# Routing operands moved into the columns that the attention products leave free in their PSUM banks, and routing constants issued one by one

## The chip, the cores and the metric

The kernel runs on one core of one Trainium2 chip. The metric is the device time of one execution in microseconds (us); the kernel before takes 656.65 us, the median of three runs (655.53, 656.65, 656.81). TensorE (PE) does the matmuls, VectorE (DVE) and ScalarE (ACT) the elementwise work, GpSimd (POOL) part of the pooling and the indirect DMAs, SyncE (SP) issues the other DMAs.

## What is computed

Two layers, one behind the other. Attention with keys and values that are averaged in groups of 8, for 8 batches, 8 heads, 576 positions of 64 elements; then a mixture of experts (MoE) in which every one of the 4608 tokens goes to its best expert of 8.

```python
k_p = k.reshape(B, H, Sp, pool, D).mean(axis=3)          # 576 -> 72 keys
v_p = v.reshape(B, H, Sp, pool, D).mean(axis=3)
scores = scale * np.matmul(q, k_p.transpose(0, 1, 3, 2))
attn = softmax(scores)
x = (attn @ v_p) with the heads side by side             # 4608 x 512
logits = x @ w_gate + modality_bias[modality_id]         # 4608 x 8
e_idx = np.argmax(logits, axis=1)
gate_w = softmax(logits)[np.arange(N), e_idx]
for e in range(8):
    mask = e_idx == e
    h = np.maximum(x[mask] @ w1[e], 0.0)                 # 512 -> 1024
    out[mask] = gate_w[mask, None] * (h @ w2[e])         # 1024 -> 512
```

## The kernel before

**Attention.** The tokens are 36 tiles of 128, worked off in 20 steps (`steps`): four steps out of five take two tiles, and the mixed step takes one tile that holds the last 64 tokens of two batches. The main loop (L882 to L955) issues the steps as a software pipeline. In step n it finishes the tiles of step n - 1 (`old`), makes the second half of the scores of step n and the first half of step n + 1. The parts are

- `q_pe`, `q_act` (L480, L494): the queries are transposed by TensorE and copied by ScalarE.
- `s_pe` (L498), `s_dve` (L518), `s_act` (L529): the scores in PSUM; VectorE takes their maximum `mx` (L522) and the difference `sb` (L525); ScalarE takes the exponentials (L537, L538).
- `t_pe`, `t_act`, `t4_pe`, `t4_act` (L540 to L563): the probabilities are transposed and copied to `pt` and `pt4`. In program order `s_act(n, 0)` stands ahead of `t4_act(n - 1)` on ScalarE.
- `a_pe` (L565): the products with the pooled values (L579 and L583), for four heads into each of two PSUM banks `av0` and `av1`. Each value has a column of ones and the gate's weights beside it, so that the sums and the gate's logits come out too. 292 of a bank's 512 columns are used.
- `x_dve` (L585): for each bank u the sum (L599), its reciprocal (L601), the normalised output `xb` (L603) and the logits of each head `lg` (L605).
- `v_gate` (L370): the gate columns of the values, two TensorE lines (L378, L379) and three VectorE lines.

Functions that a step owes now and then (the pooling of the next batch, the splits of the weights, the start of a routing group) hang in `hook_0` to `hook_3` by step.

**Routing.** After every nine tiles a group is routed: `route(g)` (L635) is a list of about 24 small VectorE operations, and then nine `arow` (L706), which compare a row 0 to 127 (`iota_b`) with each token's place. In it are `lgr` (the logits, L653 to L662), `ex` on ScalarE (L659), the count `dc` (L680), a chain of matmuls that adds up the places (`pe`, L671 to L675), and `rs` (L695 or L698). These operations wait in a list `drip`, and `gap(n)` (L458) issues the next n of them at fixed places inside `s_dve` and `x_dve`; `release()` issues one that holds TensorE work. Behind group 0 comes `first_expert` (L709), behind group 1 `early_table` (L746). Group 3 is routed after the attention, in the first slot of the MoE; its `arow` stand in `late[0, 5]` (L1062).

**Constants.** `routing_constants_2` (L422) makes 11 VectorE constants in one block at the end of step 3 (L950): `idt`, `idw`, `mf` (L430, which reads the modality words `mod`), `mq`, `bias_all` and `b1` (which read `mb`), `w8`. Both are loaded by SP in step 1 (`load_routing`, L398 to L403); GpSimd pools keys and values at the same time (L296 to L298).

**MoE.** Up to 27 slots of 256 tokens, 19 of them filled here. `first` (L159) makes a block of hidden units in a PSUM tile `hp` (TensorE L163, ScalarE L165, VectorE L167 for the residual `hlo`), `second` (L1101) the output products (L1108). fp32 operands are split into a high and a low part, with three products. The tiles `hp` take the banks of `av0` and `av1` (L970). At the end of slot 0, at f = 7, `first_next` (L1124) makes the first block of slot 1 in `hp[0]`.

All tiles are under a framework that puts semaphore waits between engines wherever their accesses of a tile depend on each other; for PSUM it does so by bank.

Of the kernel before, what the change touches and what calls it, by code (L numbers as in the profile page):

```python
# [30 lines left out]
def kernel(  # L31
# [152 lines left out]
    with ExitStack() as actx:  # L184
# [237 lines left out]
        def routing_constants_2():  # L422
            mod, mb, ids, idt = RC["mod"], RC["mb"], RC["ids"], RC["idt"]
            nc.vector.tensor_single_scalar(idt, ids, 6, op=ALU.logical_shift_right)
            nc.vector.tensor_copy(idw[:, 0, :], idt)
            nc.vector.tensor_single_scalar(idt, ids, 63, op=ALU.bitwise_and)
            nc.vector.tensor_scalar_add(idw[:, 1, :], idt, 1.0)
# [2 lines left out]
            nc.vector.tensor_copy(mf, mod[:, :, 0])  # L430
# [3 lines left out]
            nc.vector.tensor_tensor(bias_all, mq[:, 0, :].rearrange("p (t o) -> p t o", o=1).to_broadcast([P, NT, E]),
                                    mb[:, 0:1, :].to_broadcast([P, NT, E]), op=ALU.mult)
            nc.vector.tensor_tensor(b1, mq[:, 1, :].rearrange("p (t o) -> p t o", o=1).to_broadcast([P, NT, E]),
                                    mb[:, 1:2, :].to_broadcast([P, NT, E]), op=ALU.mult)
            nc.vector.tensor_add(bias_all, bias_all, b1)

            nc.vector.tensor_scalar(w8, iota_f[:, 0:E], -1.0, float(E), op0=ALU.mult, op1=ALU.add)  # L440
# [124 lines left out]
        def a_pe(t):  # L565
# [69 lines left out]
        def route(g):  # L635
# [6 lines left out]
            m2 = small("m2", g, [P, n])
            sm = small("sm", g, [P, n])
            dc = small("dc", g, [P, E])
            rs = small("rs", g, [P, n, E])
            rk = small("rk", g, [P, n])
            rki = small("rki", g, [P, n], I32)
            rkm = small("rkm", g, [P, n], I32)
            rkf = small("rkf", g, [P, n])
# [55 lines left out]
            for i in range(n):  # L705
                add(lambda i=i: V.tensor_scalar(arow[:, t0 + i, :], iota_b, rkf[:, i:i + 1], None, op0=ALU.is_equal))  # L706
            return ops

        def first_expert():  # L709
# [172 lines left out]
        for n in range(N + 1):  # L882
# [354 lines left out]
```

## Time and profile before

| | before |
|---|---|
| median of three runs | 656.65 us (655.53 to 656.81) |
| the profiled execution | 655.7 us, span 654.0 us |
| mean granted TensorE clock | 0.983 |
| busy PE, DVE, ACT, POOL | 94%, 67%, 52%, 30% |
| first output product of the MoE (L1108) | at 202 us |
| ranges of TensorE waits of 1.8 us or more between 45 and 206 us | 3.02, 1.86, 1.83, 1.86, 2.04 us |

The span runs from the first to the last instruction; the execution's time is 1.7 us longer. Times below are microseconds from the span's start. In a row of single instructions stand start, duration, engine, line, operation, output <- input, elements, the count of instructions in the row and, in brackets, the wait just before it and what ended it. In a row of a stretch stand the busy times of PE, PEld (the weight load), DVE, ACT and POOL, then the clock that TensorE was granted (1.00 is full).

### The profile page before, as it was taken

The page shows a single profiled execution, that of the slowest core. Times are in us where ns is not written, and L with a number is a line of the kernel's source. Part 1 is how long each engine was busy: PE and PEld are TensorE (multiplying, and loading weights), DVE is VectorE, ACT ScalarE, POOL GpSimd, SP SyncE. Part 2 cuts the span into 40 slices and gives each one's busy share as a digit, 9 for nine tenths or more (in the row PEclk, how much of TensorE's full clock was granted, in tenths as well). Part 3 has the DMA queues.
Part 4 walks back from the last instruction along what each step waited for, and adds up shares of the span by engine and source line. Part 5 has one row for each costly group of instructions (what it writes and reads, how often), then busy time and mean ns, then how long its engine had stood idle before and what let it go on. Part 6 is the DMA issues. An engine that isn't in the chain of part 4 may idle for free.

```text
span 654.0 us, 12681 instructions
## 1 busy us (share of the span) xinstructions
PE 616.0 (94%) x4313; PEld 558.6 (85%) x4313; DVE 438.6 (67%) x963; ACT 340.9 (52%) x625; POOL 193.6 (30%) x239
## 2 busy tenths in 40 slices
PE   4898898899799999999999999999999999999993
PEld 3697798789698999999999999999999999999982
DVE  4878888999987666665665666566566656656530
ACT  2674574478451354454555555555555555555530
POOL 5698744661100121311211212320221221122121
PEclk9998898899999999999999999999999999999997
DMA  9999978473411821202102253201215410120120
GB/s 253 289 279 353 354 220 285 143 241 108 126 28 58 258 82 51 67 1 67 55 15 64 88 185 117 65 33 35 67 50 176 163 55 17 51 66 17 51 72 15
DMA packets 63484, 77.15 MB, mean 118 GB/s; under 512 B 15535, under 2 KB 42159, under 8 KB 63408
## 3 DMA queue, kind: packets, MB, share of 16 engines
q1 hardware_dynamic: 57168, 55.98, 27.9%
q0 software_dynamic: 6240, 20.26, 9.6%
q8 instruction: 36, 0.59, 0.4%
q14 instruction: 40, 0.33, 0.2%
HBM read 119.94 MB, written 19.71 MB: 214 GB/s over the span
## 4 chain that ended last, share of the span: by engine, by line
PE 73%; DVE 12%; DMA 8%; issue 4%; ACT 1%; SPq 0%; POOL 0%; POOLq 0%; DVEq 0%; ACTq 0%
PE op L1108 27%; PE hp L163 27%; DMA out_dram<-ob,sidx 7%; PE av L579 4%; PE sc L515 3%; PE xt L154 2%; PE av L583 2%; DVE mx L522 2%; DVE sb L525 2%; PE ph L163 2%; PE pp L544 1%; PE pq L490 1%; DVE hl L139 1%; PE ptab L1014 1%; DMA k<-in_k_dram 1%
## 5 line engine op out<-in xcount | busy, mean ns | idle before, releaser
L136 ACT CAST hl<-raw 128x1024 fp32r<-128x1024 f32 x138 | 144.8, 1049 | 143.0 <-PE op L1108 140.0
L163 PE MATMUL hp<-xh,hl 128*128 128x256 f32 x1152 | 186.0, 284 | 0.6 <-issue 0.6
L163 PEld LDWEIGHTS hp<-xh,hl 128*128 128x128 f32 x1152 | 166.1, 189 | 11.6 <-issue 1.0
L139 DVE TENSOR_TENSOR hl<-raw,hl 128x1024 fp32r<-128x1024 f32 x144 | 174.9, 1216 | 0.0
L1108 PE MATMUL op<-hl,hh 128*128 128x512 f32 x556 | 174.2, 394 | 0.0
L1094 POOL DMA_INDIRECT out_dram<-ob,sidx x38 | 52.7, 1387 | 376.6 <-DVE ob L1090 267.1
L167 DVE SCALAR_TENSOR_TENSOR hlo<-hp,hh 128x256 fp32r<-128x256 f32 x139 | 58.9, 424 | 139.8 <-ACT hh L165 134.9
L1108 PE MATMUL op<-hl,hlo 128*128 128x512 f32 x278 | 108.8, 392 | 0.0
L1108 PEld LDWEIGHTS op<-hl,hh 128*128 128x128 f32 x556 | 95.2, 189 | 12.2
L163 PE MATMUL hp<-xl,hl 128*128 128x256 f32 x576 | 92.0, 282 | 0.0
L165 ACT ACTIVATE hh<-hp 128x256 fp32r<-128x256 f32 x139 | 53.4, 384 | 49.6 <-PE hp L163 47.6
L163 PEld LDWEIGHTS hp<-xl,hl 128*128 128x128 f32 x576 | 79.0, 190 | 0.0
L1108 PEld LDWEIGHTS op<-hl,hlo 128*128 128x128 f32 x278 | 52.2, 188 | 11.8
L579 PE MATMUL av<-vw,pt 128*128 128x146 f32 (+1 forms) x320 | 52.7, 306 | 1.8 <-DVE lg L605 1.5
L143 POOL DMA_INDIRECT xg<-xs,gidx x40 | 43.5, 1088 | 17.7 <-issue 9.2
L579 PEld LDWEIGHTS av<-vw,pt 128*128 128x128 f32 (+1 forms) x320 | 42.2, 190 | 4.1 <-DVE lg L605 2.8
L515 PE MATMUL sc<-kt,qt 128*128 128x144 f32 x256 | 40.0, 303 | 1.9 <-DVE sb L525 1.8
L522 DVE TENSOR_REDUCE mx<-sc 128x8 f32<-128x576 f32 (+1 forms) x40 | 27.7, 693 | 17.6 <-ACT pt L563 10.9
L515 PEld LDWEIGHTS sc<-kt,qt 128*128 128x128 f32 x256 | 35.8, 203 | 2.5 <-issue 2.0
L157 DVE TENSOR_TENSOR xl<-xt,xh 128x512 fp32r<-128x512 f32 x38 | 24.6, 686 | 17.6 <-ACT xh L156 17.6
L549 ACT COPY pt<-pp 128x512 f32<-128x512 f32 x36 | 21.1, 585 | 29.1 <-PE pp L544 28.5
L583 PE MATMUL av<-vw,pt 128*128 128x146 f32 (+1 forms) x160 | 31.2, 298 | 0.5 <-ACT pt L563 0.5
(226 smaller groups left out, 725.7 us busy)
## 6 DMA issues: line engine op xcount, KB each, us to landing
raw<-in_moe_w_dram SPq DMA_DIRECT2D x304, 256.0 KB
xs<-xb SPq DMA_DIRECT2D x16, 528.0 KB
k<-in_k_dram SPq DMA_DIRECT2D x7, 1024.0 KB
v<-in_v_dram SPq DMA_DIRECT2D x7, 1024.0 KB
q<-in_q_dram SPq DMA_DIRECT2D x6, 1024.0 KB
q<-in_q_dram SPq DMA_DIRECT2D x4, 512.0 KB
v<-in_v_dram SPq DMA_DIRECT2D x16, 128.0 KB
xs<-xb SPq DMA_DIRECT2D x8, 132.0 KB
```

The lines of the kernel that those rows point to most:

```text
L136: nc.scalar.copy(hl[f][:, 0, :], raw[f])
L139: eng.tensor_sub(hl[f][:, 1, :], raw[f], hl[f][:, 0, :].bitcast(F32))
L143: nc.gpsimd.indirect_dma_start(out=xgs[(2 * s + tt) % len(xgs)], out_offset=None, in_=xs[0:rows, :], in_offset=IndirectOffsetOnAxis(idx[:, ...
L163: nc.tensor.matmul(ph, hl[f][:, w, d * P:(d + 1) * P], x[:, d, :], start=(n == 0 and d == 0), stop=(n == 2 and d == ND - 1))
L165: nc.scalar.activation(hh, ph, AF.Relu)
L167: nc.vector.scalar_tensor_tensor(hlo, ph, 0.0, hh.bitcast(F32), op0=ALU.max, op1=ALU.subtract)
L515: nc.tensor.matmul(dst, qt[:, i, :], kt[b % NB][:, :, h * SPL:(h + 1) * SPL], start=True, stop=True)
L522: nc.vector.reduce_max(mx, scv, axis=AX.X)
L579: nc.tensor.matmul(av[u][hs, 2 * VC * gg:2 * VC * (gg + 1)], pt[:, c, hs], vw[y][:, c].rearrange("p a x -> p (a x)"), start=(gg == 0), sto ...
L583: nc.tensor.matmul(dst4[hs], pt4[:, hs], v4[y][:, 2 * u:2 * u + 2, :], start=False, stop=True)
L1094: nc.gpsimd.indirect_dma_start(out=out[:, :], out_offset=IndirectOffsetOnAxis(idx.bitcast(U32), 0), in_=ob, in_offset=None, bounds_check=N ...
L1108: nc.tensor.matmul(o[tt], l[:, ts_], hl[f][:, w, D:2 * D], start=(f == 0 and n == 0), stop=(f == NF - 1 and n == 2))
```

## The change

`av0` and `av1` are allocated once and stay (`av_bank`); the products and the MoE's `hp` use them directly. A helper `place(u, shape)` cuts tiles from columns 292 to 511 of bank u. In `av0` then lie `iota_q` (fp32, in place of the bf16 `iota_b`; copied by VectorE from `iota_f` at the start, where GpSimd cast it before), `m2`, `sm`, `rk`, `rki`, `rkm` and `dc`; in `av1` lie `e0oh`, `lg` (the group's logits, `lgr` before), `rs`, `rot` and the early table's `s0`; its `b1` uses the columns of `rs`. `first_expert` gets a second tile `rots` in SBUF and one copy more. The eleven constants become a list that `hook_0` hangs behind `drip` in step 3.

```diff
+    AVW = 4 * VC
+    av_bank = [ps_av.tile([P, 512], F32, name=f"av{u}") for u in range(2)]
+    taken = [AVW, AVW]
+    def place(u, shape, dt=F32):
+        n = 1
+        for x in shape[1:]:
+            n *= x
+        c = taken[u]
+        taken[u] += n
+        assert taken[u] <= 512
+        a = av_bank[u][:, c:c + n]
+        if dt != F32:
+            a = a.bitcast(dt)
+        return a if len(shape) == 2 else a.rearrange("p (t e) -> p t e", e=shape[2])
...
-    iota_b = cp.tile([P, P], BF16, name="iota_b")
-    nc.gpsimd.tensor_copy(iota_b, iota_f)
+    iota_q = place(0, [P, P])
+    nc.vector.tensor_copy(iota_q, iota_f)
...
-    e0oh = cp.tile([P, E], F32, name="e0oh")
+    e0oh = place(1, [P, E])
...
         def routing_constants_2():
...
+            return [
+                lambda: V.tensor_single_scalar(idt, ids, 6, op=ALU.logical_shift_right),
...
+                lambda: V.tensor_copy(mf, mod[:, :, 0]),
...
-            av = [ps_av.tile([P, 512], F32, tag=f"av{u}", name=f"av_{t}_{u}") for u in range(2)]
+            av = av_bank
...
+        RQ = {k: place(1, [P, GT, E]) for k in ("lg", "rs")}
+        RQ.update((k, place(0, [P, GT])) for k in ("m2", "sm", "rk"))
+        RQ.update((k, place(0, [P, GT], I32)) for k in ("rki", "rkm"))
+        RQ.update(dc=place(0, [P, E]))
...
+            lg, rs, m2, sm, dc, rk, rki, rkm = (RQ[k] for k in ("lg", "rs", "m2", "sm", "dc", "rk", "rki", "rkm"))
...
-                add(lambda i=i: V.tensor_scalar(arow[:, t0 + i, :], iota_b, rkf[:, i:i + 1], None, op0=ALU.is_equal))
+                add(lambda i=i: V.tensor_scalar(arow[:, t0 + i, :], iota_q, rkf[:, i:i + 1], None, op0=ALU.is_equal))
...
-            rot = ap.tile([P, E], F32, name="rot")
+            rot = place(1, [P, E])
+            rots = ap.tile([P, E], F32, name="rots")
...
-                lambda: V.tensor_add(rot, rot, t8),
-                lambda: V.tensor_tensor(lmat, rot.rearrange("p (o e) -> p o e", o=1).to_broadcast([P, E, E]),
+                lambda: V.tensor_add(rots, rot, t8),
+                lambda: V.tensor_copy(rot, rots),
+                lambda: V.tensor_tensor(lmat, rots.rearrange("p (o e) -> p o e", o=1).to_broadcast([P, E, E]),
                                         rot.rearrange("p (e o) -> p e o", o=1).to_broadcast([P, E, E]), op=ALU.is_lt),
...
-            s0 = ap.tile([P, T], F32, name="s0")
+            s0 = place(1, [P, T])
...
-            b1 = ap.tile([P, C, T], BF16, name="b1")
+            b1 = RQ["rs"].rearrange("p t e -> p (t e)").rearrange("p (c t) -> p c t", c=C)
...
+        at(hook_0, 3, lambda: drip.extend(routing_constants_2()))
...
-            if n == 3:
-                routing_constants_2()
...
-    hp = [ps_av.tile([P, 512], F32, tag=f"av{i}", name=f"hp{i}") for i in range(2)]
+    hp = av_bank
```

The order of instructions moves in one place. On VectorE, around the end of step 3, the constants stood in a block between `sb` of step 4's first half and `mx` of its second half (the last two constants are left out; what a row waits for stands in brackets, DMAHW are DMA queues):

```order
L605 TENSOR_TENSOR lg_429<-av_1_641,r_1_674 128x32
L522 TENSOR_REDUCE mx_0_694<-sc_0_682 128x8 [waits PE_49]
L525 TENSOR_TENSOR sb_0_696<-sc_0_682,mx_0_694 128x576 [waits DVE_49]
L424 TENSOR_SCALAR idt<-ids 128x36
L425 CAST idw<-idt 128x36 [waits DVE_49]
L426 TENSOR_SCALAR idt<-ids 128x36 [waits DVE_49]
L427 TENSOR_SCALAR idw<-idt 128x36 [waits DVE_49]
L430 CAST mf<-mod 128x36 [waits DMAHW2_49,DMAHW7_49,DMAHW1_49,DMAHW0_49]
L432 TENSOR_SCALAR mq<-mf 128x36 [waits DVE_49]
L432 TENSOR_SCALAR mq<-mf 128x36
L434 TENSOR_TENSOR bias_all<-mq,mb 128x288 [waits DMAHW3_49,DVE_49]
L436 TENSOR_TENSOR sc_107<-mq,mb 128x288 [waits DVE_49]
```

On the same engine and at the same place, the changed kernel issues (`av_72` is bank `av1`; lines are the changed file's own, 26 higher here in the tile functions):

```order
L625 TENSOR_SCALAR r_1_670<-av_72 128x4 [waits PE_49]
L457 CAST mf<-mod 128x36 [waits DMAHW2_49,DMAHW7_49,DMAHW1_49,DMAHW0_49]
L627 RECIPROCAL r_1_670<-r_1_670 128x4 [waits DVE_49]
L458 TENSOR_SCALAR mq<-mf 128x36 [waits DVE_49]
L629 TENSOR_TENSOR xb_169<-av_72,r_1_670 128x256 [waits DVE_49]
L631 TENSOR_TENSOR lg_427<-av_72,r_1_670 128x32
L459 TENSOR_SCALAR mq<-mf 128x36
L450 TENSOR_TENSOR bias_all<-mq,mb 128x288 [waits DMAHW3_49,DVE_49]
L548 TENSOR_REDUCE mx_0_694<-sc_0_682 128x8 [waits PE_49]
L450 TENSOR_TENSOR sc_107<-mq,mb 128x288 [waits DVE_49]
L462 TENSOR_TENSOR bias_all<-bias_all,sc_107 128x288 [waits DVE_49]
L551 TENSOR_TENSOR sb_0_698<-sc_0_682,mx_0_694 128x576
```

`mf`, with its wait for the four loads of the modality words, has moved from behind `sb` of step 4 into the normalisation of the tile before it; four earlier constants stand above these rows, in the second half of step 3.

Elsewhere the order stays, and the waits change. On TensorE, at the end of slot 0 of the MoE, the first block of slot 1 (`hp`) before:

```order
L1108 MATMUL op_1_2881<-hl_2412,h_6_2773 128x512 x3
L163 MATMUL hp_2884<-xh_2875,hl_1766 128x256 [waits DMAHW3_49,DMAHW2_49,DMAHW7_49,DMAHW1_49,Activation_49]
L163 MATMUL hp_2884<-xh_2875,hl_1766 128x256 x3
L163 MATMUL hp_2884<-xl_2876,hl_1766 128x256 [waits DVE_49]
L163 MATMUL hp_2884<-xl_2876,hl_1766 128x256 x3
```

And in the changed kernel on the same engine (`av_71` is bank `av0`):

```order
L1133 MATMUL op_1_2776<-hl_2329,h_6_2680 128x512 x3
L182 MATMUL av_71<-xh_2770,hl_1709 128x256 [waits DMAHW2_49,DMAHW3_49,DMAHW1_49,DMAHW7_49,DVE_49,Activation_49]
L182 MATMUL av_71<-xh_2770,hl_1709 128x256 x3
L182 MATMUL av_71<-xl_2771,hl_1709 128x256 x4
L182 MATMUL av_71<-xh_2770,hl_1709 128x256 x4
```

The block's first matmul waits for VectorE now: the last VectorE instruction that touches bank `av0` ahead of it is the last `arow`, which reads `iota_q`.

More of the change, by code (lines that the diff above doesn't have):

```diff
@@ L422, in routing_constants_2, with biased @@
         def routing_constants_2():
+            V = nc.vector
             mod, mb, ids, idt = RC["mod"], RC["mb"], RC["ids"], RC["idt"]
[L424 to L427, printed above, removed]
             mf = ap.tile([P, NT], F32, name="mf")
             mq = ap.tile([P, 2, NT], F32, name="mq")
-            nc.vector.tensor_copy(mf, mod[:, :, 0])
-            for m in range(2):
-                nc.vector.tensor_single_scalar(mq[:, m, :], mf, float(m), op=ALU.is_equal)
             b1 = sc1
[L434 to L440, printed above, removed]
+            def biased(m, dst):
+                V.tensor_tensor(dst, mq[:, m, :].rearrange("p (t o) -> p t o", o=1).to_broadcast([P, NT, E]),
+                                mb[:, m:m + 1, :].to_broadcast([P, NT, E]), op=ALU.mult)
+            return [
+                lambda: V.tensor_single_scalar(idt, ids, 6, op=ALU.logical_shift_right),
+                lambda: V.tensor_copy(idw[:, 0, :], idt),
+                lambda: V.tensor_single_scalar(idt, ids, 63, op=ALU.bitwise_and),
+                lambda: V.tensor_scalar_add(idw[:, 1, :], idt, 1.0),
+                lambda: V.tensor_copy(mf, mod[:, :, 0]),
+                lambda: V.tensor_single_scalar(mq[:, 0, :], mf, 0.0, op=ALU.is_equal),
+                lambda: V.tensor_single_scalar(mq[:, 1, :], mf, 1.0, op=ALU.is_equal),
+                lambda: biased(0, bias_all),
+                lambda: biased(1, b1),
+                lambda: V.tensor_add(bias_all, bias_all, b1),
+                lambda: V.tensor_scalar(w8, iota_f[:, 0:E], -1.0, float(E), op0=ALU.mult, op1=ALU.add),
+            ]
         steps = []
@@ L638, in route @@
             sl = slice(t0, t0 + n)
-            lg = small("lgr", g, [P, n, E])
             ex = small("ex", g, [P, n, E])
+            rkf = small("rkf", g, [P, n])
             m1 = small("m1", g, [P, n])
[L642 to L649, printed above, removed]
+            lg, rs, m2, sm, dc, rk, rki, rkm = (RQ[k] for k in ("lg", "rs", "m2", "sm", "dc", "rk", "rki", "rkm"))
             V = nc.vector
```

## The prediction

> **What bounds the kernel now.** I read the page first, then TensorE's busy time and clock by stretches, then the waits and single instructions at the places where TensorE stops. The page's TensorE row and five stretches (start:end, length, busy time of PE, PEld, DVE, ACT, POOL, granted clock, DMA share, GB/s):
>
> ```profile
> PE 616.0 (94%) x4313; PEld 558.6 (85%) x4313; DVE 438.6 (67%) x963; ACT 340.9 (52%) x625; POOL 193.6 (30%) x239
> ...
> 62.00:70.00 8.00, 8.00 (x68) 7.67 (x66) 6.64 (x22) 5.89 (x17) 5.03 (x10) 1.00 1.06 352
> 70.00:80.00 10.00, 7.93 (x50) 6.15 (x49) 9.71 (x34) 3.56 (x11) 9.21 (x10) 0.83 1.06 351
> 101.00:110.00 9.00, 7.17 (x47) 6.85 (x46) 7.78 (x32) 4.44 (x11) 2.07 (x2) 0.81 0.75 255
> 172.00:182.00 10.00, 7.35 (x76) 6.51 (x76) 9.70 (x29) 2.93 (x7) 0.00 (x0) 1.00 0.17 56
> 182.00:203.00 21.00, 21.00 (x172) 20.82 (x172) 15.81 (x60) 9.58 (x24) 0.00 (x0) 1.00 0.13 40
> ```
>
> TensorE carries the time: where it is full (62 to 70, 182 to 203) a microsecond lost is a microsecond at the end. It loses time in short stretches, where VectorE is nearly full and the clock falls to about 0.8: (1 - 0.83) x 10 and (1 - 0.81) x 9 are 1.7 us of clock each. TensorE's first matmuls after its long waits (start, duration, line; in brackets the wait and its releaser):
>
> ```profile
> 54.77 0.63 PE L378 MATMUL sc<-wgb,vt 128*128 128x32 f32 x4 [3.02 <-DVE sb L525]
> 73.73 0.63 PE L378 MATMUL sc<-wgb,vt 128*128 128x32 f32 x4 [1.86 <-DVE sb L525]
> 103.10 1.64 PE L515 MATMUL sc<-kt,qt 128*128 128x144 f32 x6 [1.83 <-DVE sb L525]
> 119.24 0.63 PE L378 MATMUL sc<-wgb,vt 128*128 128x32 f32 x4 [1.86 <-DVE sb L525]
> 178.65 0.73 PE L163 MATMUL ph<-xl,hl 128*128 128x256 f32 x4 [2.04 <-DVE xl L157]
> ```
>
> I call the first four S1, S2, S3 and S4. Why VectorE is late there (per line: ns minimum/median/maximum; then one GpSimd instruction):
>
> ```profile
> L654 DVE TENSOR_TENSOR lgr<-lgr,bias_all x4: 232/1314/2400, 70.6 to 204.6; 128x72 f32<-128x72 f32 x4
> ...
> 70.57 2.34 POOL L296 TENSOR_TENSOR v<-v 128x1024 f32<-128x1024 f32 x1
> ...
> L706 DVE TENSOR_SCALAR arow<-iota_b,rkf x36: 218/243/3051, 100.7 to 215.2; 128x128 bf16<-128x128 bf16 x36
> L603 DVE TENSOR_TENSOR xb<-av,r x72: 409/424/425, 27.3 to 202.6; 128x256 f32<-128x256 f32 x72
> L698 DVE TENSOR_TENSOR rs<-sc,oh x2: 222/222/222, 88.0 to 133.2; 128x72 f32<-128x72 f32 x2
> ```
>
> L654 has both inputs in SBUF and takes 232 ns or 2400: at 70.6 it stands as long as GpSimd's L296. L603, with one input in PSUM, never passes 425 ns in 72 runs, under the same GpSimd work. So operations on the moved operands should not be held at S2 to S4. The sum hangs on what their place in the products' banks and the new issue order make wait instead.
>
> **The constants (S1): +3.3.** They keep their SBUF operands, so only their places change. In order: the DMA packets of 47.5 to 48.0, then VectorE, ScalarE and TensorE.
>
> ```profile
> DMA packets 23, 0.00 MB, mean 1 GB/s; under 512 B 23, under 2 KB 23, under 8 KB 23
> ...
> 45.29 0.76 DVE L522 TENSOR_REDUCE mx<-sc 128x8 f32<-128x576 f32 x1 [0.38 <-PE sc L515]
> 46.08 0.76 DVE L525 TENSOR_TENSOR sb<-sc,mx 128x576 f32<-128x576 f32 x1
> 49.86 0.50 DVE L430 CAST mf<-mod 128x36 f32<-128x36 int32 x1
> 52.20 0.46 DVE L438 TENSOR_TENSOR bias_all<-bias_all,sc 128x288 f32<-128x288 f32 x1
> ...
> 46.90 0.64 ACT L537 ACTIVATE pe<-sb 128x512 f32<-128x512 f32 x1
> 47.58 0.56 ACT L563 COPY pt<-sc 64x128 f32<-64x128 f32 x2
> ...
> 48.14 0.41 PE L583 MATMUL av<-vw,pt 128*128 128x146 f32 x2
> 51.15 0.60 PE L490 MATMUL pq<-ident,q 128*128 128x128 f32 x4
> ```
>
> Before, mf (L430) runs at 49.86, when the modality words are there. Now it stands inside the normalisation of step 3, which VectorE reaches at about 44.6 (before, it ended there 0.38 ahead of mx at 45.29). The words travel in packets under 512 B, and the last of these still move in the slice 47.5 to 48.0, so mf waits until about 48.2. Behind it in VectorE's queue stand the rest of that normalisation, five more constants and mx and sb of step 4. From mf to L438 before are 52.66 - 49.86 = 2.8 us; with 0.6 for the rest of the normalisation (L603's 0.42 and small ones) and 1.5 for mx and sb (0.76 as L525, twice), sb ends at about 53.1 instead of 46.84: 6.3 late. ScalarE takes the exponentials of sb (L537) before its copy L563, so that copy is 6.3 late too, and TensorE's L583, which reads it, goes at about 54.4 instead of 48.14. From there to the end of L490 before are 51.75 - 48.14 = 3.6 us; TensorE passes L490 at 58.1, where before it had waited until 54.77. That is +3.3. With no GpSimd in the way three wide constants take 0.46 each, as L438, and three narrow ones no more than L698's 0.22: 2.0 instead of 2.8, and the price is +2.5; held by as much again, +4.1. If the words came by 44.6, the constants would fill waits such as the 0.38 before mx, and TensorE's wait would shrink by something between 0.4 and its 3.02; I take -1.2, nearer the first. The slow clock that followed the old wait follows the new one instead.
>
> **Group starts (S2, S4): -0.2 each.** The count dc (VectorE), and TensorE's next products:
>
> ```profile
> 76.48 0.28 DVE L680 TENSOR_REDUCE dc<-oh 128x8 f32<-128x72 bf16 x1
> ...
> 74.83 0.77 PE L579 MATMUL av<-vw,pt 128*128 128x146 f32 x4
> ```
>
> L654 falls from 2.40 to 0.23: 2.2 us earlier on VectorE, and the matmuls of L378 go 1.9 earlier. But dc now lies in the bank that the products at 74.83 write, and they wait for it. It moves from 76.76 to 74.6, less than 0.2 us before those products went anyway. TensorE's wait moves from before L378 to behind it. If the clock then holds, up to 1.9 each.
>
> **The first expert (S3): -3.0.**
>
> ```profile
> 95.23 1.27 DVE L724 TENSOR_TENSOR t<-e0oh,iota_f 128x8 f32<-128x8 f32 x1
> 97.99 0.67 DVE L727 TENSOR_SCALAR rot<-iota_f,e 128x8 f32<-128x8 f32 x1
> 98.69 0.65 DVE L728 TENSOR_SCALAR t<-rot 128x8 f32<-128x8 f32 x1
> 100.72 1.57 DVE L706 TENSOR_SCALAR arow<-iota_b,rkf 128x128 bf16<-128x128 bf16 x2
> ```
>
> At 0.2 us each, the first three give back 2.0 and the two arows 1.1; the added copy takes 0.1. So sb is 3.0 earlier. TensorE's wait of 1.83 goes but for 0.5 in which the products ahead wait for an arow, and the slow clock behind it, 1.7, goes too. Bounds: 1.3 if the clock falls all the same, 3.5 if nothing waits.
>
> **Group 1's arows: -1.2.**
>
> ```profile
> 138.69 3.21 DVE L706 TENSOR_SCALAR arow<-iota_b,rkf 128x128 bf16<-128x128 bf16 x2
> ```
>
> VectorE gains 2.8. None of TensorE's long waits lies there, so I take less than half; bounds 0 and 2.8.
>
> **Groups 2 and 3: +0.4, +1.5, +2.8.** GpSimd is nearly idle by then, so nothing is gained, and new waits remain (TensorE and ScalarE at group 2's start; then rs, TensorE's products, the residual and TensorE's transposes; then the MoE's first hidden block and the last arows):
>
> ```profile
> 162.32 0.69 PE L579 MATMUL av<-vw,pt 128*128 128x146 f32 x4
> 164.38 0.26 ACT L659 ACTIVATE ex<-lgr 128x72 f32<-128x72 f32 x1 [2.56 <-DVE m L655]
> ...
> 179.18 0.22 DVE L695 TENSOR_TENSOR rs<-sc,adjv 128x72 f32<-128x72 f32 x1
> 181.09 0.42 PE L583 MATMUL av<-vw,pt 128*64 128x146 f32 x4
> 184.97 0.42 DVE L167 SCALAR_TENSOR_TENSOR h<-ph,h 128x256 fp32r<-128x256 f32 x1
> 185.79 0.60 PE L544 MATMUL pp<-ident,pe 128*128 128x128 f32 x4
> ...
> 212.92 0.63 PE L163 MATMUL hp<-xh,hl 128*128 128x256 f32 x4
> 213.87 1.54 DVE L706 TENSOR_SCALAR arow<-iota_b,rkf 128x128 bf16<-128x128 bf16 x9
> ```
>
> The products at 162.32 wait for ex, which reads the logits in their bank and ends at 164.64. That holds TensorE 2.3, but VectorE is the bound here; its next read of that bank must wait for these products (0.69 long): +0.4 (0 to 1.1). At 179.18 rs must now wait for the products that end at 181.51: 2.3 on VectorE. The transposes that wait for the residual went 0.4 after its end at 185.39, so at most 1.9 late; VectorE is idle a quarter of 182 to 203, so up to 1.5 of the six microseconds between may swallow it: +1.5 (0.4 to 1.9), near the top, since that idle time need not fall there. At 212.92 the MoE's hidden block takes the bank in which iota_q lies, so TensorE waits for the last arow, which ends at 215.41. From L698 to L603 an element from PSUM costs (409 - 222) / (256 - 72) = 1.02 ns, so an arow from there takes 222 + 56 x 1.02 = 279 ns, 0.06 over L706's minimum; nine of them end 0 to 0.5 later: +2.8 (2.5 to 3.0). The slow clock followed four of the five waits above (not the last, in whose stretch it is 1.00); I charge half of 1.7, +0.8 (0 to 1.7). [...]
>
> Everything else is hidden: iota_q's copy lies under the first loads, GpSimd's missing cast under its own queue, the early table's wait under the wait at 162.32.
>
> **Sum**: 3.3 - 0.2 - 0.2 - 3.0 - 1.2 + 0.4 + 1.5 + 2.8 + 0.8 = +4.2. The profiled run took 655.7 (span 654.0), so 659.9; from the median of 656.65 it is 660.85. I take 660.4, and add 0.5 to the profiled run's sums below alike.
>
> **The rivals.**
> Faster: the release of dc at S2 and S4. If it comes so early that TensorE's wait there falls well under the 1.83 us after which the clock fell, the clock holds and each place gives 3.5 instead of 0.2: 4.2 - 6.6 = -2.4, 653.8. For it: VectorE is 2.2 earlier. Against it: dc stands last in the group's first block.
> No change: the modality words come before mf. Then S1 is -1.2 instead of +3.3: -0.3, 655.9. Against it: the packets of 47.5 to 48.0.
> The change doesn't do what it says: an operand in PSUM waits for GpSimd all the same. S2 to S4 and group 1 give nothing: 4.2 + 4.6 = +8.8, 665.0. L603's maximum speaks against it.
> PSUM is dearer for VectorE: some 23 small operations of groups 2 and 3, on a path there, each cost the 0.06 more that the arow's estimate gives: +1.4, 661.8. Against it: 72 elements take 222 ns with PSUM (L698) and 232 without (L654's minimum). [...]
>
> **The numbers.** Chances: forecast 0.60 (657.5 to 663), no loss at dc 0.14, early words 0.12, PSUM still held 0.07, PSUM dearer 0.07. The range 655.2 to 665.0 leaves out the faster rival and the forecast's tails, 0.19. About 0.2%, 1.3 us, is what a measurement of this kernel can tell from no change. Faster is the first rival and 0.03 of tail, 0.17; same the early words and 0.03, 0.15; slower the rest, 0.68.
>
> **What would show it.** Right: mf starting at about 48 after an idle VectorE; TensorE idle from 48 to about 54; L654 and the arows never above 0.5 us; TensorE's first hidden block behind the last arow. Wrong: mf at 45 without a wait, clock 1.00 in the stretches of S2 and S4, or the hidden block of slot 0 starting at once.

## The result and the profile after

The changed kernel takes 664.18 us, the median of four runs (662.88 to 666.5); the kernel before takes 656.51 beside it (655.53 to 656.81). The ratio is 1.0114, interval 1.0077 to 1.0151: slower by 7.7 us, where 3.75 were forecast. The profiled execution took 664.43 us, span 662.7, mean granted clock 0.980.

Single runs scatter with the clock: in 35 runs beside the first experiments the kernel before took 651.49 to 661.15 us, the fastest at 0.986, the slowest at 0.975. So the ratios carry the verdicts, and the traces, one for each kernel, the causes. In experiment 7 two of ten runs (667.57 and 667.67) were slow ones and are left out.

The page's engine row of the changed kernel: TensorE has the same 4313 instructions and 2.6 us less busy time than before, VectorE 10.8 less. The kernel does not work more, it waits more.

```profile
PE 613.4 (93%) x4313; PEld 555.9 (84%) x4313; DVE 427.8 (65%) x965; ACT 340.5 (51%) x625; POOL 193.2 (29%) x238
```

TensorE's first matmuls after its new waits, from the timeline of the changed kernel (start, duration; the wait and what ended it in brackets):

```profile
55.11 0.85 PE L609 MATMUL av<-vw,pt 128*128 128x146 f32 x2 [5.38 <-ACT pt L589]
79.22 0.52 PE L605 MATMUL av<-vw,pt 128*128 128x146 f32 x2 [2.15 <-DVE av L703]
104.19 0.77 PE L605 MATMUL av<-vw,pt 128*128 128x146 f32 x4 [0.97 <-DVE arow L729]
122.61 0.64 PE L605 MATMUL av<-vw,pt 128*128 128x146 f32 x3 [2.15 <-DVE av L703]
140.72 0.74 PE L605 MATMUL av<-vw,pt 128*128 128x146 f32 x4 [1.36 <-DVE arow L729]
155.12 0.77 PE L605 MATMUL av<-vw,pt 128*128 128x146 f32 x4 [1.41 <-DVE b L800]
165.55 0.77 PE L605 MATMUL av<-vw,pt 128*128 128x146 f32 x4 [1.47 <-ACT ex L682]
189.25 0.66 PE L570 MATMUL pp<-ident,pe 128*128 128x128 f32 x4 [1.50 <-DVE h L186]
220.69 1.20 PE L182 MATMUL av<-xh,hl 128*128 128x256 f32 x4 [3.30 <-issue]
```

All but the eighth are matmuls that write one of the two banks. In order they wait for the constants (S1), for `dc` at S2 (L703), for an `arow` at S3, for `dc` at S4, for an `arow` of group 1, for the early table's `b1` (the program calls the tile b), for group 2's exponentials, for the residual behind `rs`, and for the last `arow`. The same trace on VectorE: `mf`, the `sb` behind it, `dc` at S2, `rs`, and the last nine `arow`:

```profile
49.60 0.18 DVE L457 CAST mf<-mod 128x36 f32<-128x36 int32 x1 [3.46 <-DMA mod<-in_moe_modality_id_dram]
53.34 0.74 DVE L551 TENSOR_TENSOR sb<-sc,mx 128x576 f32<-128x576 f32 x1
78.88 0.29 DVE L703 TENSOR_REDUCE av<-oh 128x8 f32<-128x72 bf16 x1
183.41 0.24 DVE L718 TENSOR_TENSOR av<-sc,adjv 128x72 f32<-128x72 f32 x1 [2.29 <-PE av L609]
218.19 2.40 DVE L729 TENSOR_SCALAR arow<-av,rkf 128x128 bf16<-128x128 f32 x9
```

`mf` stands idle 3.46 us for the modality words. `dc` ends at 79.17, and the products follow at 79.22. The last `arow` ends at 220.59, and the MoE's hidden block follows at 220.69: the profile puts that wait down to "issue", but it ends 0.1 us after the `arow`, the VectorE instruction that the matmul waits for. The two lines that GpSimd held before, minimum/median/maximum in ns:

```profile
L677 DVE TENSOR_TENSOR av<-av,bias_all x4: 241/241/242, 75.2 to 208.9; 128x72 f32<-128x72 f32 x4
L729 DVE TENSOR_SCALAR arow<-av,rkf x36: 320/342/352, 103.8 to 220.3; 128x128 bf16<-128x128 f32 x36
```

They went up to 2400 and 3051 before. What the change is good for is there: both lines now read from the banks, and GpSimd holds neither any more, at 242 and 352 ns at most. Last, TensorE's clock by stretches (the column behind the five engines): S2, what follows it, S3, S4, and the MoE's start.

```profile
70.00:80.00 10.00, 7.70 (x61) 6.53 (x60) 8.30 (x34) 5.98 (x17) 9.13 (x13) 0.99 1.06 347
80.00:93.00 13.00, 13.00 (x116) 12.04 (x116) 8.06 (x31) 6.31 (x16) 3.45 (x4) 0.87 0.62 168
101.00:110.00 9.00, 7.68 (x62) 7.30 (x62) 8.49 (x40) 4.53 (x11) 5.85 (x7) 1.00 0.76 256
117.00:126.00 9.00, 6.71 (x56) 5.35 (x56) 7.60 (x34) 3.96 (x13) 8.57 (x10) 1.00 0.50 151
216.00:220.00 4.00, 1.39 (x6) 0.78 (x5) 3.86 (x14) 0.00 (x0) 0.00 (x0) 0.98 0.00 1
220.00:224.00 4.00, 3.31 (x14) 3.24 (x15) 1.61 (x6) 0.37 (x1) 0.00 (x0) 0.50 0.97 284
224.00:228.00 4.00, 4.00 (x20) 3.48 (x19) 2.62 (x12) 0.80 (x3) 1.02 (x1) 0.67 1.02 327
```

The kernel before at S4 and at the MoE's start:

```profile
117.00:126.00 9.00, 7.00 (x45) 6.24 (x44) 8.49 (x34) 3.36 (x11) 7.70 (x8) 0.81 0.29 74
212.00:216.00 4.00, 4.00 (x26) 3.55 (x25) 3.83 (x17) 0.44 (x2) 0.00 (x0) 1.00 0.06 16
```

In this trace the slow clock is gone at S3 and S4, has moved behind the new wait at S2, and is new at the MoE's start.

**Where the time went.** The table takes the same TensorE matmul in a kernel's trace and in the trace of before, and how much later it starts (the median of five neighbours), at 27, 59, 80, 105, 124, 148, 171, 197 and 217 us of before; the last point is a ScalarE instruction at 625. A column is what is lost (+) or gained (-) between two points. The first row is the forecast's own terms; its MoE start is the wait of 2.8 and the 0.8 for the clock. The kernels are numbered as the experiments below. Where a wait lies near a point, the cut between two columns shifts by some tenths with the neighbours that are taken; in row 7 a wait of 4.54 lies at the point itself, and only its sum of S1 and S2 can be read.

| us | to 27 | S1 | S2 | S3 | S4 | group 1 | table, group 2 | rs | MoE start | MoE rest | sum |
|---|---|---|---|---|---|---|---|---|---|---|---|
| forecast | 0 | 3.3 | -0.2 | -3.0 | -0.2 | -1.2 | 0.4 | 1.5 | 3.6 | 0 | 4.2 |
| changed kernel | 1.3 | 2.8 | 0.0 | -2.0 | -1.5 | -0.8 | 2.0 | 2.5 | 6.2 | -1.9 | 8.6 |
| 1 block | 1.1 | -0.1 | 0.0 | -2.0 | 0.3 | -0.1 | 2.0 | 2.5 | 5.1 | -1.8 | 6.8 |
| 2 banks swapped | 0.6 | 1.2 | 0.0 | -2.0 | -0.6 | -0.1 | 2.0 | 2.5 | 0.7 | -1.9 | 2.3 |
| 3 late groups in SBUF | -0.3 | 4.1 | -0.1 | -2.0 | -1.5 | -0.8 | 0.9 | 0.0 | 0.0 | 1.4 | 1.8 |
| 4 both (1 and 3) | -0.1 | -1.8 | 0.0 | -2.0 | 0.3 | -0.1 | 0.9 | 1.6 | 0.0 | 1.2 | 0.1 |
| 5 before again | 1.2 | -0.1 | 0.0 | -0.1 | 0.1 | 0.0 | 0.0 | 0.0 | 0.0 | 0.0 | 1.2 |
| 6 changed, unused `iota_b` | 0.8 | 3.1 | -0.3 | -1.8 | 0.3 | 0.1 | 2.0 | 2.5 | 5.1 | -1.9 | 9.8 |
| 7 singly in step 4 | -0.8 | -0.2 | 1.4 | -2.0 | -0.3 | -0.3 | 2.4 | 2.4 | 4.9 | -1.9 | 5.6 |
| 8 few operands in PSUM | -0.3 | 0.5 | -2.3 | -1.9 | -3.4 | -0.2 | 0.6 | 0.0 | 0.0 | 1.5 | -5.6 |
| 9 as 8, 96 bytes | 0.0 | -1.0 | -2.7 | -1.9 | -3.4 | -0.2 | 0.6 | -0.2 | 0.0 | -1.8 | -10.5 |
| 10 changed, 64 bytes | -1.0 | 3.5 | 0.0 | -2.0 | -1.5 | -0.8 | 2.0 | 2.5 | 6.2 | -0.8 | 8.2 |
| 11 as 9, block in step 4 | -0.3 | -4.9 | 3.6 | -1.9 | -3.4 | -0.2 | 0.6 | -0.2 | 0.0 | -1.1 | -7.7 |
| 12 before, 64 bytes | 0.7 | -0.4 | 0.0 | -0.1 | 0.1 | 0.0 | 0.0 | -0.2 | 0.0 | -1.9 | -1.9 |

Row 5 tells what a column means: the kernel before against itself differs by 1.2 in the first 27 us and by 0.1 after that. So the first column belongs to the run, not to the kernel, and nothing shows the 1.3 of the changed kernel's profiled run to be an effect of the change (in the other traces that issue the constants in step 3 it is -1.0 to 0.8); the profiled runs differ by 8.7 us, the medians by 7.7.

### The profile page after: what moved, and what is told of

It is laid out like the page before. It is cut to its first block, busy times and chain, and to the rows that moved or that the text cites. A ratio compares the mean times of both kernels' runs of the same rounds, so it can differ in the third digit from the quotient of the medians.

```text
span 662.7 us, 12678 instructions
## 1 busy us (share of the span) xinstructions
PE 613.4 (93%) x4313; PEld 555.9 (84%) x4313; DVE 427.8 (65%) x965; ACT 340.5 (51%) x625; POOL 193.2 (29%) x238
## 4 chain that ended last, share of the span: by engine, by line
PE 73%; DVE 10%; DMA 9%; issue 5%; SPq 1%; POOL 1%; ACT 1%; POOLq 0%; DVEq 0%
PE op L1133 27%; PE av L182 27%; DMA out_dram<-ob,sidx 7%; PE av L605 5%; PE sc L541 3%; PE av L609 2%; PE xt L173 2%; DVE sb L551 2%; PE pp L570 2%; PE pq L516 1%; DVE xb L629 1%; PE ph L182 1%; DVE mx L548 1%; PE ptab L1039 1%; DMA k<-in_k_dram 1%
## 5 line engine op out<-in xcount | busy, mean ns | idle before, releaser
L182 PE MATMUL av<-xh,hl 128*128 128x256 f32 x1152 | 185.6, 284 | 4.2 <-issue 4.2
L182 PEld LDWEIGHTS av<-xh,hl 128*128 128x128 f32 x1152 | 166.3, 191 | 15.4 <-issue 5.0
L186 DVE SCALAR_TENSOR_TENSOR hlo<-av,hh 128x256 fp32r<-128x256 f32 x139 | 58.9, 423 | 142.0 <-ACT hh L184 133.5
L182 PE MATMUL av<-xl,hl 128*128 128x256 f32 x576 | 92.0, 282 | 0.0
L184 ACT ACTIVATE hh<-av 128x256 fp32r<-128x256 f32 x139 | 53.2, 383 | 52.1 <-PE av L182 49.9
L182 PEld LDWEIGHTS av<-xl,hl 128*128 128x128 f32 x576 | 78.8, 191 | 0.0
L541 PE MATMUL sc<-kt,qt 128*128 128x144 f32 x256 | 38.2, 294 | 0.0
L609 PE MATMUL av<-vw,pt 128*128 128x146 f32 (+1 forms) x160 | 31.3, 299 | 5.9 <-ACT pt L589 5.9
```

Of the source, the lines that this page charges most:

```text
L182: nc.tensor.matmul(ph, hl[f][:, w, d * P:(d + 1) * P], x[:, d, :], start=(n == 0 and d == 0), stop=(n == 2 and d == ND - 1))
L184: nc.scalar.activation(hh, ph, AF.Relu)
L186: nc.vector.scalar_tensor_tensor(hlo, ph, 0.0, hh.bitcast(F32), op0=ALU.max, op1=ALU.subtract)
L541: nc.tensor.matmul(dst, qt[:, i, :], kt[b % NB][:, :, h * SPL:(h + 1) * SPL], start=True, stop=True)
L609: nc.tensor.matmul(dst4[hs], pt4[:, hs], v4[y][:, 2 * u:2 * u + 2, :], start=False, stop=True)
```

## The experiments

**1. The constants as a block again.** The changed kernel, with only the constants put back behind step 3.

```diff
-        at(hook_0, 3, lambda: drip.extend(routing_constants_2()))
...
+            if n == 3:
+                for fn in routing_constants_2():
+                    fn()
```

> The changed kernel with the eleven constants back in one block at the end of step 3. Theory (mf's wait for the modality words holds the whole step): the 5.38 us wait of TensorE before L609 goes, the old one of about 3 us before the gate columns comes back, and the kernel is 2.7 us faster than the changed one, about 661.5. Rival (the constants' places cost nothing, the lost time there is the slow clock that came by chance): within 0.8 us of the changed kernel's 664.2, the clock in 45 to 62 still about 0.8.

662.01 us, median of 12 runs; ratio 1.0093 (1.0064 to 1.0123). The medians are 2.2 apart and the two intervals overlap, so the trace has to show the cause. In the table S1 goes from 2.8 to -0.1; S4, group 1 and the MoE's start move too, by 1.8, 0.7 and -1.1; at S4 it is the clock, which is 0.62 in that stretch here. The wait at S1 is that of before again, 2.48 us instead of 5.38:

```profile
55.71 0.63 PE L397 MATMUL sc<-wgb,vt 128*128 128x32 f32 x4 [2.48 <-DVE sb L551]
```

So issuing the constants singly in step 3 is what costs at S1. Over the five traces that issue them in step 3 (the changed kernel, 2, 3, 6, 10), S1 is 2.8, 1.2, 4.1, 3.1 and 3.5, mean 2.9. `mf` waits 3.46, 1.76, 3.20, 2.19 and 3.67 us in them: the price goes with the wait for the words, though not one to one.

**2. The hidden block in the other bank.** The first block of slot 1 writes `av1` instead of `av0`, whose `iota_q` the last `arow` read.

```diff
-    hp = av_bank
+    hp = av_bank[::-1]
```

> The changed kernel with the two banks of the MoE's hidden blocks exchanged, so that the first block of slot 1 goes into the bank that holds no iota_q. Theory (TensorE waits 3.3 us for the last arow and then runs 6 us at half clock): both go, 6.3 us faster, about 657.9. Rival 1 (only the wait counts, the clock would have fallen anyway): 3.3 faster, 660.9. Rival 2 (the wait is hidden by what comes behind it): within 0.8 of 664.2.

659.73 (12 runs); 1.0050 (1.0027 to 1.0074). From the same engine's timeline, and the stretch behind it:

```profile
219.89 0.74 PE L182 MATMUL av<-xh,hl 128*128 128x256 f32 x4 [0.43 <-DVE arow L729]
```

```profile
220.00:224.00 4.00, 4.00 (x29) 3.74 (x30) 3.61 (x16) 1.56 (x3) 1.02 (x1) 1.00 0.95 279
```

A wait of 0.43 in place of 3.30, and 1.00 in place of 0.50: both terms go together, 6.2 to 0.7 in the table. The median is 1.8 above the 657.9 of the theory and 1.2 below the 660.9 of the first rival, so it is the one trace that decides between them. The mechanism is shown; its price in the forecast, 3.6, was too low, since the slow clock behind the wait costs about as much as the wait. By the stretches of the changed kernel above, TensorE's busy time times the clock that is missing, it is 3.31 x 0.50 + 4.00 x 0.33 = 3.0 us, and the table leaves 6.2 - 3.3 = 2.9.

**3 and 4. Groups 2 and 3 with their operands in SBUF.** The third kernel keeps everything of the change for groups 0 and 1 only; the fourth also has the block of the first.

```diff
+            RG = RQ if g < 2 else {
+                "lg": small("lgr", g, [P, n, E]), "rs": small("rs", g, [P, n, E]), "dc": small("dc", g, [P, E]),
...
+            iota_g = iota_q if g < 2 else iota_b
```

> The changed kernel with the routing operands of groups 2 and 3 back in SBUF (iota_b for their arows too); groups 0 and 1, the early table and the constants stay as changed. Theory (from group 2 on GpSimd is idle, so PSUM gains nothing and its waits cost at the group's start, at rs and at the MoE's first block): 9.8 faster than the changed kernel, about 654.4. Rival (at group 2's start and at rs VectorE is the bound and swallows the waits): only the MoE's part, about 657.9.

> Both the block of constants and the SBUF operands of groups 2 and 3; what is left of the change are the PSUM operands of groups 0 and 1, the first expert and the early table. Theory: the prices add up, 12.5 faster than the changed kernel, about 651.7, that is 4.8 faster than the kernel before, since the waits on GpSimd at the first expert and at group 1's arows stay away. Rival (what the PSUM operands give there is given back by their own waits): the time of the kernel before, 656.5, within 1.

660.05 (12 runs), 1.0069 (1.0037 to 1.0101), and 658.17 (12 runs), 1.0029 (0.9994 to 1.0064): 5.7 and 6.5 us above what was expected. The waits do what was expected. In the table, `rs` (fourth kernel aside) and the MoE's start are 0.0, and group 2 loses 0.9 instead of 2.0. TensorE's waits of the third kernel from 150 to 228 us:

```profile
PE ph L182 <- DVE xl L176: 2.0, 1, 2.0
PE av L605 <- DVE b L807: 1.4, 1, 1.4
PE av L605 <- DVE lg L631: 0.9, 1, 0.9
PE pp L570 <- DVE xl L176: 0.6, 1, 0.6
PE sc L535 <- DVE sb L551: 0.3, 1, 0.3
```

Neither `ex` nor `rs` nor the `arow` is in it. What failed is outside the theory: the rest of the MoE, where the two kernels' order is the same, loses 1.4 and 1.2, and the changed kernel gains 1.9 there. That is 3.3 and 3.1 of the difference; experiments 5, 6, 9, 10 and 12 are about it. The remaining 2.4 and 3.4 us were not settled. In the fourth kernel's trace a slow clock costs 1.7 around 180 us, behind a wait that the kernel before has too:

```profile
175.00:185.00 10.00, 9.05 (x71) 8.55 (x72) 7.92 (x29) 2.21 (x6) 0.00 (x0) 0.83 0.14 30
```

That is the 1.6 under `rs`. In the kernel before, after the same wait of 2.04, this stretch runs at 1.00:

```profile
175.00:185.00 10.00, 7.96 (x84) 7.39 (x83) 9.38 (x30) 3.54 (x9) 0.00 (x0) 1.00 0.25 83
```

**5 and 6. Is the MoE's rate chance, or `iota_b`'s 256 bytes?** The kernel before once more, unchanged, for its trace; and the changed kernel with an `iota_b` that nothing reads.

```diff
+    iota_b = cp.tile([P, P], BF16, name="iota_b")
+    nc.gpsimd.tensor_copy(iota_b, iota_f)
```

> The kernel before, once more, for a second trace of it. If the speed of the MoE part (TensorE full, clock 1.00) belongs to the kernel, its slots run as in the first trace, within 0.3 us from 250 us to the end; if it differs by chance from execution to execution, by 1 us or more. The product of span and granted clock should be 642.7 within 2, as the mean of the 35 timed runs of this kernel has it.

> The changed kernel with the bf16 row iota_b (256 bytes a partition) still allocated and cast by GpSimd, but not read. Theory (the MoE's matmuls run a little faster or slower by where their operands lie in SBUF, and the change moved them by taking iota_b out): the MoE part from 250 us on becomes 1.5 to 3 us longer than the changed kernel's, as in the runs that kept iota_b; span times clock 648.5 becomes 650 to 651.5. Rival (chance): within 0.5 of the changed kernel's MoE part, span times clock 648.5.

656.97 in one run, with the MoE at the same rate as in the first trace (0.0 in the table); and 664.5 (4 runs), 1.0116 (1.006 to 1.0173), with the changed kernel's rate (-1.9). So the rate belongs to the program and not to the run, and 256 bytes more do nothing to the changed kernel's.

**7. The constants singly, but a step later.** By then the modality words are there.

```diff
-        at(hook_0, 3, lambda: drip.extend(routing_constants_2()))
+        at(hook_0, 4, lambda: drip.extend(routing_constants_2()))
```

> The changed kernel with the constants issued singly one step later, when the modality words have landed. Theory (the words, not the single issue, cost the time in step 3): no wait for them on VectorE, TensorE's wait before L609 under 0.6 us, span times clock 3 to 4 lower than the changed kernel's 648.5, so at or below the 647.0 of the block. Rival (single constants are held by GpSimd again and again and hold the step themselves): 647 or above, with a TensorE wait of 2 us or more in step 4 or 5.

662.57 (eight runs), 1.0097 (1.0058 to 1.0136). `mf`, now at 50.75, waits no more, and TensorE's wait of 5.38 before L609 is gone; but now two constants stand between `mx` and `sb` while GpSimd works (VectorE, GpSimd, then TensorE's matmul behind this `sb`):

```profile
51.75 0.45 DVE L450 TENSOR_TENSOR bias_all<-mq,mb 128x288 f32<-128x288 f32 x1
52.12 0.74 DVE L548 TENSOR_REDUCE mx<-sc 128x8 f32<-128x576 f32 x1
52.79 3.30 DVE L450 TENSOR_TENSOR sc<-mq,mb 128x288 f32<-128x288 f32 x1
56.12 1.40 DVE L462 TENSOR_TENSOR bias_all<-bias_all,sc 128x288 f32<-128x288 f32 x1
57.44 0.74 DVE L551 TENSOR_TENSOR sb<-sc,mx 128x576 f32<-128x576 f32 x1
```

```profile
53.43 2.33 POOL L315 TENSOR_TENSOR v<-v 128x1024 f32<-128x1024 f32 x1
55.84 1.36 POOL L316 TENSOR_TENSOR v<-v 128x512 f32<-128x512 f32 x1
```

```profile
58.33 2.26 PE L541 MATMUL sc<-kt,qt 128*128 128x144 f32 x8 [4.54 <-DVE sb L551]
```

The second L450 and L462 end 0.3 us after L315 and L316, and take 3.30 and 1.40 us, where the first L450 takes 0.45. TensorE waits 4.5 us for this `sb`. S1 and S2 together cost 1.2 here, 2.8 in the changed kernel, -0.1 with the block: the rival holds. Its number alone, 647 or above, would not have told the two apart, since the product of span and clock (which takes most of the clock's scatter out: the eight runs lie 8.5 us apart, their products 3.2) is 647.0 on the mean of the eight runs; its sign, a wait of 2 us or more, does. Singly is dearer in either step, by the words in one and by GpSimd in the other.

**8. Only what no TensorE wait hangs on stays in PSUM.** The fourth kernel, and `m2`, `sm`, `dc` of groups 0 and 1 and the early table's `s0` and `b1` in SBUF too. In PSUM remain the logits, `rs`, `rk`, `rki`, `rkm`, `iota_q` of groups 0 and 1, `rot` and `e0oh`.

```diff
+            RG = {**RQ, **{k: small(k, g, [P, n]) for k in ("m2", "sm")}, "dc": small("dc", g, [P, E])} if g < 2 else {
...
-            s0 = place(1, [P, T])
+            s0 = ap.tile([P, T], F32, name="s0")
...
-            b1 = RQ["rs"].rearrange("p t e -> p (t e)").rearrange("p (c t) -> p c t", c=C)
+            b1 = ap.tile([P, C, T], BF16, name="b1")
```

> The block of constants, SBUF operands for groups 2 and 3, and for groups 0 and 1 also m2, sm and dc, and the early table's s0 and b1, in SBUF; in PSUM stay lg, rs, rk, rki, rkm, rot, e0oh and iota_q of groups 0 and 1. Theory (dc and the early table's b hold the products without being held by GpSimd themselves): the two waits of 2.1 us before the products of the group starts and the one of 1.4 go; span times clock falls from the 643.9 of the kernel with SBUF operands in groups 2 and 3 to about 638.5, the time to about 652.5, below both kernels. Rival (the products wait as long for lg, which stays in PSUM): 643 and 657.

650.14 (6 runs), 0.9900 (0.9858 to 0.9942): faster than both. The product of span and clock, 641.0 on the mean of the six runs, is 2.5 above what was expected; the time is 2.4 lower all the same, because the clock is higher, at 0.987 to 0.990. The waits for `dc` and `b1` are gone, and the clock holds at S2 and S4:

```profile
70.00:80.00 10.00, 9.43 (x75) 7.83 (x74) 9.42 (x40) 5.49 (x16) 9.45 (x12) 1.00 1.06 348
117.00:126.00 9.00, 8.83 (x85) 8.38 (x87) 7.78 (x35) 6.56 (x17) 3.67 (x5) 1.00 0.49 134
```

S2 and S4 give 2.3 and 3.4 us, where they gave 0.0 and 1.5: the forecast's faster rival had put 3.5 on each, which S4 reaches and S2 does not, and its condition, that `dc` no longer holds TensorE, is what the change does not meet. `m2` and `sm` left the bank together with `dc`; that it is `dc` that counts is read from the two waits for L703, not from a run of its own.

**9, 10 and 12. The place of the MoE's operands in SBUF.** Among the traces so far the MoE's rate went with the address at which the weights `hl`, the tokens `xh1` and the hidden values `hh` begin, counted modulo 128 bytes: 64 before, 0 in the changed kernel and its variants 1, 2, 6 and 7, 32 in 3, 4 and 8. So unused bytes are put ahead of them: 96 in the eighth kernel, 64 in the changed one, 64 in the one before.

```diff
+    pad = cp.tile([P, 24], F32, name="pad")
+    nc.gpsimd.memset(pad, 0.0)
```

> The eighth kernel with 96 unused bytes in SBUF, so that the MoE's operands (weights hl, tokens xh1, hidden values hh), which began 32 bytes past a multiple of 128 there, begin at one, as they do in the changed kernel. Theory: the MoE's matmul spacing goes by that offset; the MoE from 250 us on runs 3.0 us faster (95th and 99th percentile of the spacing 235 and 236 ns instead of 236 and 240), and 650.1 becomes about 647. Rival: the spacing belongs to something else in the program; then nothing moves.

> The changed kernel with 64 unused bytes in SBUF: the MoE's operands begin 64 bytes past a multiple of 128, as in the kernel before, instead of at one. Nothing else is changed. Theory: the MoE takes the rate of the kernel before, 1.7 us more (spacing 236 and 238 ns), about 665.9. Rival: 664.2, spacing 235 and 236.

> The kernel before with 64 unused bytes in SBUF: the MoE's operands begin at a multiple of 128 bytes, as in the changed kernel. Theory: the MoE runs 1.7 us faster, 654.8, with a spacing of 235 and 236 ns. Rival: nothing moves, 656.5 and 236 and 238.

The ninth takes 647.16 (5 runs), 0.9844 (0.9813 to 0.9875), the fastest of all; the twelfth 652.94 (6 runs), 0.9923 (0.9896 to 0.9950); the tenth 663.97 (4 runs), 1.0125 (1.0075 to 1.0175). Mean time in ns from one matmul's start to the next from 250 us on, in matmuls of 256 columns with the high part of the tokens, and the 95th and 99th percentile over all matmuls:

```
kernel   begins at (mod 128, mod 256)   256 columns   95%, 99%   MoE rest against before
before          64,  64                 120.92        236, 238    0.0
12               0, 128                 119.51        235, 236   -1.9
changed          0, 128                 119.42        235, 236   -1.9
10              64, 192                 119.99        235, 236   -0.8
8               32,  32                 120.79        236, 240   +1.5
9                0, 128                 119.44        235, 236   -1.8
```

That the place changes the rate is shown by 12 against before (-1.9, expected -1.7) and by 9 against 8 (3.3 faster, expected 3.0). All three kernels with unused bytes have the same added write to them, and the tenth gets slower with it, so it is not that write. Row 11 of the table, at the ninth's addresses, has -1.1 in the last column because it loses 0.8 at 228 us, in a wait for a load; from 250 us on it gains the ninth's 1.8. The rule modulo 128 fell: by it the tenth should lose 1.7 against the changed kernel, and it loses 1.1, with the percentiles of the twelfth. A rule modulo 256 would fit all six rows, but only 128 occurs in more than one of them; it was made after them, and no run tests it. Nor is shown which of the operands it is.

**11. The block a step later.** The ninth kernel with `if n == 4` in place of `if n == 3`.

> The ninth kernel with the constants as a block at the end of step 4 instead of step 3. In the eighth kernel TensorE waits 2.7 us there for sb, which stands behind the block, and runs at half clock for about 6 us behind it; a step later VectorE has waits of 2.35 and 1.16 us and GpSimd one of 3.5 us. Theory: the wait goes, the half clock with it (2.7 and 2.5 to 3), less what VectorE's lateness costs anew a step later (0 to 2.5): about 643.5. Rival: the block makes the same wait there, 647.

649.82 (5 runs), 0.9889 (0.9856 to 0.9921): slower than the ninth. The wait at 54 us goes (S1 is -4.9), and a longer one comes at 64, at half clock after that:

```profile
64.08 1.34 PE L605 MATMUL av<-vw,pt 128*128 128x146 f32 x4 [4.79 <-DVE lg L631]
```

```profile
62.00:68.00 6.00, 3.92 (x15) 3.40 (x16) 5.41 (x19) 1.19 (x4) 1.05 (x2) 0.50 1.08 354
```

S1 and S2 together are -1.3 in the eleventh and -3.7 in the ninth. The rival was too mild. The likely reason, which no run tests, is that VectorE's idle time a step later, 2.35 and 1.16 us, is TensorE's lead there and no room for a block that takes six microseconds.

## Why the prediction came out as it did

The direction was right, and 664.18 lies in the range of 655.2 to 665.0, near its upper end; the size forecast, 3.75, was half of the 7.7 that came. That the time lies in the range is in part luck: the MoE's operands moved in SBUF, which was not foreseen, and without the 1.9 us that this gained the median would be near 666.1, above the range. The four signs that were to show it right are all there: `mf` starts after an idle VectorE (3.46 us; at 49.60, forecast 48, and 1.3 of that is the run's), TensorE stands still behind it until 55.11 (forecast 54), L654 and the `arow` (now L677 and L729) stay at 0.24 and 0.35 us, and the MoE's first hidden block follows the last `arow`. One of the signs against it is there in part: in the stretch of S4 the clock is 1.00, as the faster rival has it. It is so in this trace and not in that of the first kernel, which waits the same 2.1; at S2 the slow clock lies behind 80 us.

- **Constants.** Right, by the mechanism named: the words, then `mf`, then everything behind it on VectorE. 2.8 against 3.3, and 2.9 on the mean of five traces. The block in experiment 1 gives -0.1.
- **S2.** Right: the wait of 1.86 before the gate columns becomes one of 2.15 behind them, for `dc`. 0.0 against -0.2.
- **S4.** The same wait of 2.15, but the clock stayed at 1.00: -1.5 against -0.2. In the traces of 1, 4 and 6 it is +0.3. In all seven traces with the same operands there (the changed kernel, 1, 2, 3, 6, 7, 10) it is -1.5 three times and -0.6 to 0.3 otherwise, and the fourth has 0.3 too. So this is the run, and the forecast's "if the clock then holds" is the condition that decides: the 1.3 better than forecast are luck.
- **S3.** -2.0 against -3.0, in every trace with the change. The operations are no longer held (L748 takes 0.17 us where L724 took 1.27, L751 0.23 where L727 took 0.67) and the clock holds, at 1.00, but the wait for an `arow`, put at 0.5, is 0.97, and a second one of 0.35 follows at 108 us.
- **Group 1.** -0.8 against -1.2; -0.3 to 0.1 in five other traces. The prediction had no wait here, but TensorE waits 1.36 for an `arow` at 140.72, by the same mechanism as at S3.
- **Group 2 and the early table.** 2.0 against 0.4; a step of the prediction failed here. The prediction hid "the early table's wait under the wait at 162.32". It does not lie there: it comes before it, at 155.12, with 1.41 us of its own, and the 1.47 for `ex` come on top. Experiment 3, with `ex` in SBUF, leaves 0.9; experiment 8, with the table in SBUF too, still 0.6, and where these come from stays open.
- **rs.** The mechanism and its first numbers held: 2.29 on VectorE (2.3), and the transposes 1.7 later by the table's reckoning (at most 1.9), of which 1.50 are TensorE's wait. But VectorE's idle time swallowed nothing: 0.9 more come at 195.02, where TensorE waits 0.68 for ScalarE's copy `pt` and the kernel before shows no such wait, and the term is 2.5, above its bound of 1.9.
- **The MoE's start.** The wait is 3.3 (2.8 forecast, 3.0 at most); an `arow` from PSUM takes 320 ns at least, 102 more than before, not 61 more. The term that was mis-sized most is the clock: 0.8 stood for the half of 1.7, and behind this wait it cost up to 3.0. Wait and clock are 6.2 here and 4.9 to 6.2 in five traces.
- **Not foreseen.** The MoE's operands moved in SBUF when `iota_b` and the small tiles left it: -1.9, by no intention of the change. And 1.3 in the first 27 us of the profiled run, which is the run's.

Together: 4.2 + 1.3 - 0.5 + 0.2 + 1.0 - 1.3 + 0.4 + 1.6 + 1.0 + 2.6 - 1.9 = 8.6.

The rivals: the words were late, so the early ones are out. Neither of the two lines that GpSimd held before was held in PSUM, by the maxima of L677 and L729 (242 and 352 ns). PSUM is dearer, but by 9 to 20 ns for 72 elements (L677 241 against 232, the `rs` of L721 242 against the 222 of L698), not 60. Only the `arow` pays 102; its row also went from two bytes an element to four, and no run separates the two. The faster rival's mechanism is real and worth 4.2 us more at S2 and S4 (experiment 8), when `dc` stays out of the bank.

On the clock, the same wait of 2.04 us was followed by 0.83 in the fourth kernel and by 1.00 in the one before, and waits of 2.15 by 0.87 and by 1.00 within one trace. In the ninth kernel a wait of 1.76 us at S1 was followed by 0.73; its first matmul after the wait, and the stretch behind it, are these:

```profile
54.19 0.63 PE L397 MATMUL sc<-wgb,vt 128*128 128x32 f32 x4 [1.76 <-DVE sb L551]
```

```profile
56.00:62.00 6.00, 6.00 (x38) 5.98 (x38) 4.47 (x15) 2.79 (x7) 5.67 (x7) 0.73 1.04 375
```

So the long waits here, from 1.76 us on, carried a further 0 to 3.0 us, and how much of it came belongs to the run; what decides it is not shown.

That columns which nobody shares still tie the engines is shown by the products' waits for `dc` (2.15 us), `b1` (1.41) and an `arow` (0.97 and 1.36), none of which touches a column of the products. The waits are those of the framework, which sets them by bank; no run leaves them out, so none shows what the chip would do without them.

## What to carry to other kernels

Here the operands in PSUM escaped GpSimd (L677 takes 242 ns at most, where L654, the same sum in SBUF, took up to 2400), but with the framework's waits their bank became a lock between VectorE and whatever TensorE writes there (2.15 us for `dc`, 3.30 for the last `arow`): for each operand ask which access of that bank comes next on the other engine, and move only those for which the answer is "nothing soon". Here eight operands of the first two groups gain 7.6 us from S2 to S4, clock included (experiment 8); `dc`, the early table's tiles and the operands of the last two groups take that back. An instruction that waits for a transfer, as `mf` did for 3.46 us, belongs behind the work that TensorE needs, not among it, and a wait of TensorE as long as those above is to be charged with the clock that may fall behind it (0 to 3.0 us here).

## What the runs showed of the hardware that was not expected

- The matmuls' spacing went with where their operands begin in SBUF: 64 unused bytes make the MoE of the kernel before 1.9 us faster (119.51 ns from one matmul of 256 columns to the next against 120.92; 652.94 against 656.77 us in the medians, of which 1.9 are shown in the trace), and 96 make the eighth kernel's 3.3 us faster (119.44 against 120.79 ns). Which address counts stays open.
- The same program took 651.49 to 661.15 us, with a mean granted clock of 0.986 and 0.975 in these two runs; 0.011 of some 650 us are 7.2 of the 9.7 between them. The ninth kernel, whose TensorE waits 22.1 us up to 215 us from the start (26.2 in the kernel before, 34.4 in the changed one), stays at 0.988 to 0.990 in five runs, within 2.6 us.
